# Loads of a and b from GpSimd's queue, and a weight conversion without ScalarE's mantissa pass, in a fused RWKV-7 and cosine-unit kernel

## Chip, core and metric

The kernel runs on one core of a Trainium2 chip. The metric is the device time of one execution in microseconds (us). Before the change the median of three runs is 825.35 us (823.66 to 827.18).

## What is computed

Two blocks stand one behind the other. The first is a recurrence over 768 steps for 4 batches and 8 heads of 40 channels (`r, k, v, w, a, b`). Its output, as 3072 tokens of 320 values, goes through a unit with a hidden width of 2048.

```
for t in range(S):                      # state: (B, H, D, D), D = 40
    y[:, :, t] = einsum('bhd,bhde->bhe', rt, state)
    Sa    = einsum('bhde,bhe->bhd', state, at)
    state = state * wt[:, :, None, :] - einsum('bhd,bhe->bhde', Sa, bt) \
          + einsum('bhd,bhe->bhde', vt, kt)
x = y.transpose(0, 2, 1, 3).reshape(B * S, H * D)   # (3072, 320)
h = x @ w_in                            # w_in (320, 2048), float64 in memory
out = (h * cos(h)) @ w_out              # w_out (2048, 320), float64 in memory
```

## The kernel before, in words

**Recurrence.** The sequence is cut into 24 chunks of 32 steps. `p1(c)` prepares two chunks at once from w, a and b: transposes (`wT`, `aps`, `bT`), the reciprocal `rw` of w (L395), `bn` = b times `rw` on GpSimd (L396), and the products `nps`. From `nps` VectorE computes triangular inverses for four chunks at once, in small steps (`inv_tmp`, `inv`); for chunks 0 to 7 only the diagonal half blocks are inverted this way and TensorE joins them (`pair_first`, `pair_second`, tiles `half` and `rt`). `p2(c)` prepares one chunk from k, v, r: the copies `vp`, `rp` (L566), `kn` (L573) and `vvm` (L574) on GpSimd, transposes, the products `gram`. `main(c)` carries the state: `ch_t` (sT), `ch_q` (qps), `ch_x` (x0ps), `ch_s` (sps), `ch_z` (dps). At the end of `ch_z` VectorE adds into the state tile `qz` (L732), GpSimd multiplies it (L733) and then the output `yt` (L744); the next chunk's `ch_t` needs `qz`. `yt` goes through memory to be transposed: SP stores `xd` (L753) and, when that has landed, loads `xT` (L763, L765).

**Loads.** `load(c, names, via)` (L150 to L156) issues four transfers of 40 KB for each name, one per batch. Nearly all of it goes through SP's queue, which takes its entries in order. From chunk 4 on, w comes as a cumulated product: `ws_scan` forms it on VectorE for four chunks at once, `ws_store` writes it to `wd` (L184), and the load of w reads `wd`. The tiles of a and b of chunks 4 and 5 are those of chunks 0 and 1. k, v, r have one tile each, so the load for chunk c + 1 waits for GpSimd's copies for chunk c.

**Weights.** They are float64, and are turned to float32 in 20 tiles of 128 x 512 by `rounded` (L224 to L264). Tiles 0, 1, 6, 7, 10, 11, 16, 17 hold the rows of w_in in two groups of 128, tiles 2 and 12 its last 64 rows (the tail), the others w_out. A tile goes through four stages:
- `fetch` loads the two 32-bit words of each number (`words`, L237);
- `taken` masks the high word's mantissa (`mant`, L245) and its exponent (`expo`, L246) on VectorE, then ScalarE turns the exponent into a power of two (L249) and takes the sign (L251);
- `mantissa` adds the low word (L255, VectorE), then ScalarE adds the implicit one and scales (L258);
- `product` multiplies mantissa and power (L261, VectorE), then GpSimd multiplies by the sign (L264).

The order is written out by hand: a list `w_steps` holds, for each tile n, product of n, fetch of a later tile, mantissa of n + 1, taken of n + 2. `step` pops a few of them after each piece of the recurrence. The words live in tiles that are used elsewhere too, so a fetch waits until the tile before it there has been read.

**Order of the work.** `step` counts down a list of deferred actions (`later(n, work)` runs it n steps on), so many loads are placed by a count of steps. Dummy matmuls (`busy`, and the tiny `pad` matmuls of `shifted`, 121 ahead of chunk 0's inverse and 75 at chunk 19) stand between the pieces. Once weights are ready, pieces of the second block (`ph`, `turns`, `gT`, `po`) are put between the pieces of the recurrence, and TensorE has work throughout.

**Borrowed space.** Ahead of the weights, the buffer of w_out holds other things: b of chunks 2 and 3 in its last 1024 columns (`late_out`), and ahead of these, in `spare`, the tiles `half0` (1024 columns) and `rn0` (512 columns) for the joining of chunk 0 to 3's inverses.

Of the kernel before, what the change touches and what calls it, by code (L numbers as in the profile page):

```python
# [9 lines left out]
F32 = mybir.dt.float32  # L10
I32 = mybir.dt.int32
U32 = mybir.dt.uint32
ALU = mybir.AluOpType
ACTF = mybir.ActivationFunctionType
# [6 lines left out]
def kernel(  # L21
# [43 lines left out]
    nc = tc.nc  # L65
    B, H, S, D = r.shape
    P, C, DP = 128, 32, 64
    HH = H // 2
    NCH = S // C
    DM, DFF = moe_w_in.shape  # L70
    NF = DFF // P
# [18 lines left out]
    def kept(name, shape, n=1, fill=None, part=lambda t: t, on=nc.gpsimd):  # L90

        tiles = []
        for i in range(n):
            t = const.tile(shape, F32, tag=f"{name}{i}", name=f"{name}{i}")
            if fill is not None:
                on.memset(part(t), fill)
            tiles.append(t)
        return tiles
# [8 lines left out]
    src = {"r": r, "k": k, "v": v, "w": w, "a": a, "b": b}  # L107
# [5 lines left out]
    w_out_sb = const.tile([P, NF, DM], F32, tag="w_out", name="w_out_sb")  # L113
# [2 lines left out]

    late = DFF - 2 * H * DP
    late_out = w_out_sb.rearrange("p f n -> p (f n)")[:, NF * DM - 2 * H * DP :]
    spare = w_out_sb.rearrange("p f n -> p (f n)")[:, NF * DM - 2 * H * DP - 3 * P * 4 : NF * DM - 2 * H * DP]
    half0 = spare[:, : 8 * P].rearrange("p (n t) -> p n t", t=C)  # L120
    rn0 = spare[:, 8 * P :].rearrange("p (n t) -> p n t", t=C // 2)
    nc.gpsimd.memset(half0[:, :, C // 2 :], 0.0)
    nat = {}
    for n, fill in (("w", 1.0), ("a", 0.0), ("b", 0.0)):
        for i in range(4):
# [24 lines left out]
    def load(c, names, via=nc.sync):  # L150
        for n in names:
            for i in range(B):
                at_c = src[n][i, :, c * C : (c + 1) * C, :]
                if n == "w" and c >= 4:
                    at_c = wd[c // 4][i, :, c % 4]
                via.dma_start(nat[n, c][blk[i], :, :D], at_c.rearrange("h t d -> t h d"))  # L156
# [51 lines left out]
    bn_b = kept("bn", [P, H, DP], 7, 0.0, padding)  # L208
    kn_b = kept("kn", [P, H, DP], 2, 0.0, padding)

    by_in = kept("by_in", [P, 1], 1, 0.5 / math.pi)[0]
    by_out = kept("by_out", [P, 1], 1, 2.0 * math.pi)[0]
    to_bits = kept("to_bits", [P, 1], 1, (127.0 - 1023) * 2**23)[0]


# [5 lines left out]
    WID = 512  # L221
    first_done, second_done = [], []

    def rounded(m, dst, src, by, by_sb):  # L224

        pool, tag = (
            ((sb2, "gT"), (sb2, "gT"), (sb1, "nt"), (sb1, "u"), (sb1, "inv"))[m % 5]
            if m < 10 else ((sb1, "nt"), (sb1, "u"), (sb1, "inv"))[(m - 10) % 3]  # L230
        )
        t = {}

        def fetch():
            t["words"] = pool.tile([P, WID, 2], I32, tag=tag, name="words")
            for rows, cols, part in src:
                nc.sync.dma_start(  # L237
                    t["words"][rows, cols].rearrange("p n w -> p (n w)"), part.bitcast(I32)
                )

        def taken():
            hi = t["words"][:, :, 1]
            t["mant"] = sb2.tile([P, WID], I32, tag="mant", name="mant")
            t["expo"] = sb2.tile([P, WID], I32, tag="expo", name="expo")
            nc.vector.tensor_scalar(t["mant"], hi, 0xFFFFF, None, ALU.bitwise_and)  # L245
            nc.vector.tensor_scalar(  # L246
                t["expo"], hi, 20, 0x7FF, ALU.logical_shift_right, ALU.bitwise_and
            )
            nc.scalar.activation(t["expo"], t["expo"], ACTF.Relu, bias=to_bits, scale=2.0**23)  # L249
            t["sign"] = sb2.tile([P, WID], mybir.dt.bfloat16, tag="sign", name="sign")  # L250
            nc.scalar.activation(t["sign"], hi, ACTF.Sign)  # L251

        def mantissa():
            frac = t["mant"].bitcast(F32)
            nc.vector.scalar_tensor_tensor(  # L255
                frac, t["words"][:, :, 0].bitcast(U32), 2.0**-32, t["mant"], ALU.mult, ALU.add
            )
            nc.scalar.activation(frac, frac, ACTF.Identity, bias=by_sb, scale=2.0**-20 * by)  # L258

        def product():  # L260
            nc.vector.tensor_tensor(  # L261
                dst, t["mant"].bitcast(F32), t["expo"].bitcast(F32), ALU.mult
            )
            nc.gpsimd.tensor_tensor(dst, dst, t["sign"], ALU.mult)  # L264

        return fetch, taken, mantissa, product

    def weights():


        wide = moe_w_in.dtype != F32
        work = []

        def put(dst, src, by, by_sb):
            if wide:
                work.append(rounded(len(work), dst, src, by, by_sb))
                return

            def fetch():
                for rows, cols, part in src:  # L280
                    nc.sync.dma_start(dst[rows, cols], part)

            none = lambda: None
            work.append((fetch, none, none, lambda: nc.scalar.mul(dst, dst, by)))

        flat_out = w_out_sb.rearrange("p f n -> p (f n)")
        for j in range(NF // 4):
            cs = slice(j * WID, (j + 1) * WID)
            for i in range(2):
                put(  # L290
                    w_in_sb[:, i, cs], [(every, slice(0, WID), moe_w_in[i * P : (i + 1) * P, cs])],
                    0.5 / math.pi, by_in,
                )
            if j % 2 == 0:
                put(
                    w_in_tail[:, j : j + 2].rearrange("p j f n -> p (j f n)"),
                    [
                        (
                            full[e], slice(2 * i * P, 2 * (i + 1) * P),
                            moe_w_in[2 * P :, (4 * (j + i) + 2 * e) * P : (4 * (j + i) + 2 * e + 2) * P],  # L300
                        )
                        for i in range(2)
                        for e in range(2)
                    ],
                    0.5 / math.pi, by_in,
                )
            first_done.append(len(work))
            for o in range(0, NF * DM, WID):
                if not 4 * j * DM <= o < 4 * (j + 1) * DM:
                    continue  # L310
                parts = []
                for f in range(o // DM, (o + WID - 1) // DM + 1):
                    lo, hi = max(o, f * DM), min(o + WID, (f + 1) * DM)
                    parts.append(
                        (
                            every, slice(lo - o, hi - o),
                            moe_w_out[f * P : (f + 1) * P, lo - f * DM : hi - f * DM],
                        )
                    )
                put(flat_out[:, o : o + WID], parts, 2.0 * math.pi, by_out)  # L320
            second_done.append(len(work))
        return work

# [19 lines left out]
    def later(steps, work):  # L343
        waiting.append([steps, work])

    def step(work, of_inv=0, of_w=0, small=False):


        before = list(waiting)
        work()  # L350
        G["small"] = small
        for w in before:
            w[0] -= 1
            if w[0] == 0:
                waiting.remove(w)
                w[1]()
        for steps, n in ((inv_steps, of_inv), (w_steps, of_w)):
            for _ in range(min(n, len(steps))):
                steps.pop(0)()
# [502 lines left out]
    def p1(c):  # L862


        def first_w():
            p1_w(c)
            if c == 4:
                later(1, lambda: load(6, "w"))

        def both_a():  # L870
            p1_a(c)
            if c == 4:
                later(1, lambda: load(7, "w"))
                for i in range(2):
                    later(1, lambda i=i: load(6 + i, "ab"))
            elif c >= 2 and c + 3 < NCH:
                for m in range(6):
                    later(
                        8 + m // 3 if c == 2 else (9 if c == 6 else 2) + m, lambda m=m: load(c + 2 + m % 2, "wab"[m // 2])
                    )  # L880

        return [first_w, both_a, lambda: p1_b(c), lambda: p1_n(c)]

# [23 lines left out]
    with tc.manual_schedule():  # L907
# [46 lines left out]
        first, other = p1(0), p1(2)  # L954
        for seg in (*first[:2], *other[:2], *first[2:], *other[2:]):
            step(seg)
        for m in range(2):
            w_work[m][0]()
        scanned(1)
# [10 lines left out]
        w_work[2][0]()  # L970
        p2_in(1)
        p2_kn(1)
        N_PAD = {0: 121, 19: 75}
        shifted(N_PAD[0])
        while inv_steps:
            inv_steps.pop(0)()
# [35 lines left out]
        for c in range(NCH):  # L1012
# [6 lines left out]
            elif c == 1:  # L1019
                parts = [parts0[0], parts0[1]]  # L1020
                segs = [t, parts[0], v, q, parts[1], k, x, g, s, z]
                fill = (1, 4)
            elif c == 2:
                parts = parts0[2:]
# [107 lines left out]
```

## Time and profile before

| | |
|---|---|
| median of three runs | 825.35 us |
| the profiled execution | 821.18 us |
| its span (first to last instruction) | 819.5 us |
| granted TensorE clock, mean | 0.955 |
| TensorE matmuls busy | 756.6 us (92%) |
| VectorE busy | 484.4 us (59%) |
| ScalarE busy | 386.5 us (47%) |
| GpSimd busy | 198.5 us (24%) |
| DMA, mean | 68 GB/s |

In the profile PE is TensorE's matmuls, PEld its weight loads, DVE VectorE, ACT ScalarE, POOL GpSimd, SP SyncE. A timeline line has the start, the duration, the engine, the line of the kernel, the operation, output <- inputs, how many were merged (x4), and in square brackets the idle time of the engine before it with what ended it. `SPq` lines are the issues of transfers in SP's queue: their duration is the time in the queue, not that of the transfer. A line of the table by stretches has, for each engine, the busy time and the number of instructions, then the granted clock, the mean busy share of the 16 DMA engines and GB/s. "issue" is idle time that the profile puts down to nothing. The profile is of one execution, and its idle times belong to an engine, not to the kernel: they count only where the end of the kernel depends on them.

### The profile page before, as it was taken

To read this page: it belongs to the slowest core of one execution; us is meant where nothing else is said; L and a number is where in the kernel's file an instruction comes from. 1 tells how busy PE (TensorE), PEld (TensorE's weight loads), DVE (VectorE), ACT (ScalarE), POOL (GpSimd) and SP (SyncE) were. 2 spreads that over 40 slices of the span, in tenths; PEclk is the share of its full clock that TensorE was granted. 3 is DMA by queue.
4 is the path that set the end of the run, shared out by engine and by line. 5 is a ranking of instruction groups with operands and counts; after the bars stand their busy time and mean duration, and the time that the engine had idled before them with its cause. 6 is when DMAs were issued, how large, how long until landed. Compare 5 with 4: busy or idle time off the path is not lost.

```text
span 819.5 us, 39690 instructions
## 1 busy us (share of the span) xinstructions
PE 756.6 (92%) x17858; PEld 580.2 (71%) x17858; DVE 484.4 (59%) x1025; ACT 386.5 (47%) x720; POOL 198.5 (24%) x354
## 2 busy tenths in 40 slices
PE   3676787999899999999999999999999999999997
PEld 2653456677677777787777877777787777777775
DVE  6956667866364698454796554895445873332231
ACT  1324566654254544446345445435635435363352
POOL 5214352430214123221230330330230222201000
PEclk9856687999999999999999999999999999999999
DMA  7536554254144323334224314214220212101000
GB/s 122 126 83 177 160 143 115 45 126 73 29 103 92 67 52 61 70 90 75 54 38 71 73 59 72 53 38 68 59 40 25 45 39 51 21 19 36 19 17 16
DMA packets 183304, 55.79 MB, mean 68 GB/s; under 512 B 157152, under 2 KB 178656, under 8 KB 183136
## 3 DMA queue, kind: packets, MB, share of 16 engines
q1 hardware_dynamic: 180560, 51.95, 29.2%
q8 instruction: 140, 2.29, 1.2%
q10 hardware_dynamic: 2320, 0.98, 0.6%
q0 software_dynamic: 256, 0.33, 0.2%
q14 instruction: 28, 0.23, 0.1%
HBM read 42.07 MB, written 11.14 MB: 65 GB/s over the span
## 4 chain that ended last, share of the span: by engine, by line
PE 63%; DVE 14%; DMA 6%; ACT 5%; SPq 5%; issue 5%; POOL 2%; DVEq 0%; ACTq 0%; POOLq 0%
PE ph L101 22%; PE po L101 18%; SPq L156 4%; PE x0ps L101 3%; PE dps L101 3%; PE gram L101 3%; DVE inv_tmp L480 2%; PE vT L330 2%; DVE rw L395 2%; DVE inv L484 2%; PE nps L101 2%; PE sps L101 2%; PE qps L101 2%; DMA words<-in_moe_w_out_dram 1%; PE sT L634 1%
## 5 line engine op out<-in xcount | busy, mean ns | idle before, releaser
L101 PE MATMUL po<-w_out_sb,gT 128*128 128x320 f32 x768 | 223.2, 439 | 0.0
L101 PE MATMUL ph<-xT,w_in_sb 128*128 128x256 f32 x768 | 188.7, 391 | 2.8 <-issue 2.5
L101 PEld LDWEIGHTS po<-w_out_sb,gT 128*128 128x128 f32 x768 | 140.2, 190 | 54.2 <-issue 1.7
L101 PEld LDWEIGHTS ph<-xT,w_in_sb 128*128 128x128 f32 x768 | 141.2, 193 | 32.9 <-issue 14.9
L806 ACT ACTIVATE turns<-ph,rnd 128x512 f32<-128x512 f32 x96 | 64.1, 686 | 159.0 <-PE ph L101 158.6
L808 DVE SCALAR_TENSOR_TENSOR turns<-turns,ph 128x512 f32<-128x512 f32 x96 | 64.0, 684 | 117.4 <-ACT turns L806 117.1
L816 DVE TENSOR_TENSOR gT<-ph,turns 128x512 f32<-128x512 f32 x96 | 65.7, 686 | 37.5 <-ACT turns L813 37.5
L733 POOL TENSOR_TENSOR qz<-qz,wc 128x160 f32<-128x160 f32 x92 | 41.7, 472 | 158.3 <-DVE qz L732 157.7
L813 ACT ACTIVATE turns<-turns,half_pi 128x512 f32<-128x512 f32 x96 | 69.3, 722 | 3.1
L812 ACT ACTIVATE turns<-turns 128x512 f32<-128x512 f32 x96 | 60.2, 627 | 16.8 <-DVE turns L808 16.8
L101 PE MATMUL ph<-xT,w_in_tail 64*128 64x256 f32 x384 | 55.8, 410 | 0.0
L484 DVE TENSOR_TENSOR inv<-inv,inv_tmp 128x31 f32<-128x31 f32 (+15 forms) x124 | 50.8, 410 | 4.3
L566 POOL COPY vp<-nat_v 128x320 f32<-128x320 f32 x25 | 12.2, 486 | 160.5 <-DMA nat_v<-in_v_dram 134.4
L732 DVE TENSOR_TENSOR qz<-dps,qz 128x160 f32<-128x160 f32 x92 | 28.9, 314 | 35.6 <-PE dps L101 35.3
L480 DVE TENSOR_TENSOR inv_tmp<-u,inv 128x31 f32<-128x31 f32 (+15 forms) x124 | 48.2, 389 | 2.3
L395 DVE RECIPROCAL rw<-nat_w 128x320 f32<-128x320 f32 x20 | 42.8, 2141 | 0.0
L638 ACT COPY s<-sT 128x512 f32<-128x512 f32 x46 | 24.5, 584 | 37.1 <-PE sT L634 37.0
L101 PEld LDWEIGHTS ph<-xT,w_in_tail 64*128 64x128 f32 x384 | 33.8, 190 | 9.4 <-issue 5.5
L744 POOL TENSOR_TENSOR yt<-yt,wb 128x512 f32<-128x512 f32 x24 | 31.4, 1309 | 22.4 <-DVE yt L739 22.4
L634 PE MATMUL sT<-ident,qz 128*128 128x128 f32 x184 | 26.6, 287 | 5.6 <-POOL qz L733 2.9
L396 POOL TENSOR_TENSOR bn<-nat_b,rw 128x320 f32<-128x320 f32 x22 | 19.5, 887 | 48.8 <-DVE rw L395 41.6
L698 DVE TENSOR_TENSOR sm<-sps,su 128x128 f32<-128x128 f32 x48 | 11.7, 285 | 31.9 <-ACT sm L693 31.9
(136 smaller groups left out, 1108.4 us busy)
## 6 DMA issues: line engine op xcount, KB each, us to landing
words<-in_moe_w_in_dram SPq DMA_DIRECT2D x8, 512.0 KB
nat_k<-in_k_dram SPq DMA_DIRECT2D x96, 40.0 KB
nat_v<-in_v_dram SPq DMA_DIRECT2D x96, 40.0 KB
nat_r<-in_r_dram SPq DMA_DIRECT2D x96, 40.0 KB
xd<-yt SPq DMA_DIRECT2D x48, 80.0 KB
out_dram<-ot SPq DMA_DIRECT2D x24, 160.0 KB
nat_b<-in_b_dram SPq DMA_DIRECT2D x88, 40.0 KB
wd<-ws SPq DMA_DIRECT2D x5, 640.0 KB
```

The lines of the kernel that those rows point to most:

```text
L101: nc.tensor.matmul(o, lhsT=lhsT, rhs=rhs, start=start, stop=stop, skip_group_check=True)
L156: via.dma_start(nat[n, c][blk[i], :, :D], at_c.rearrange("h t d -> t h d"))
L395: nc.vector.reciprocal(rw, wn)
L480: nc.vector.tensor_tensor(tmp, u[:, j : j + 1, :j].to_broadcast([P, C - j, j]), x[:, j:, j : j + 1].to_broadcast([P, C - j, j]), ALU.mult,)
L484: nc.vector.tensor_tensor(x[:, j:, :j], x[:, j:, :j], tmp, ALU.subtract)
L634: nc.tensor.transpose(ps[:, i // 4, (i % 4) * P : (i % 4 + 1) * P], qz[:, i // 2, i % 2, C : C + P], ident)
L733: nc.gpsimd.tensor_tensor(z, z, wc.rearrange("p (f m b) -> p f m b", f=2, m=2)[:, :, :, bb] .unsqueeze(3).to_broadcast([P, 2, 2, D]), ALU. ...
L806: nc.scalar.activation(n, u, ACTF.Identity, bias=rnd, scale=1.0)
L808: nc.vector.scalar_tensor_tensor(n, n, -ROUND, u, ALU.add, ALU.subtract)
L812: nc.scalar.activation(n, n, ACTF.Abs)
L813: nc.scalar.activation(n, n, ACTF.Sin, bias=half_pi, scale=-2.0 * math.pi)
L816: nc.vector.tensor_tensor(gT[:, 2 * e : 2 * e + 2].rearrange("p f t -> p (f t)"), us[e], ns[e], ALU.mult)
```

## The change

- The weights: the mask also sets the implicit one (`bitwise_or` with 0x100000), so ScalarE's pass L258 falls, and its scale goes into a three-operand product on VectorE. GpSimd's multiplication by the sign moves from the end of `product` to the end of `taken`, and works on the power of two.
- The loads: a and b of chunks 4 and 5 are issued by GpSimd, 16 transfers, behind its copies for chunk 1. w of chunks 4 and 5 stays on SP and is placed 5 and 7 steps after the first piece of chunk 1, which puts it behind the words of tile 8 and of tile 9. The deferred loads that `p1(2)` set up for them fall.
- `half0` moves into the last 1024 columns of w_out's buffer (where b of chunks 2 and 3 was), and its memset on GpSimd moves behind the preparation of chunks 0 to 3. `rn0` stays where it was. Two memsets of constants fall.
- The pad ahead of chunk 0's inverse has 115 matmuls instead of 121.

```diff
-    spare = w_out_sb...[:, NF * DM - 2 * H * DP - 3 * P * 4 : NF * DM - 2 * H * DP]
-    half0 = spare[:, : 8 * P].rearrange("p (n t) -> p n t", t=C)
-    rn0 = spare[:, 8 * P :].rearrange("p (n t) -> p n t", t=C // 2)
-    nc.gpsimd.memset(half0[:, :, C // 2 :], 0.0)
+    half0 = late_out.rearrange("p (n t) -> p n t", t=C)
+    rn0 = w_out_sb...[:, NF * DM - 2 * H * DP - P * 4 : NF * DM - 2 * H * DP]
...
-            nc.vector.tensor_scalar(t["mant"], hi, 0xFFFFF, None, ALU.bitwise_and)
+            nc.vector.tensor_scalar(
+                t["mant"], hi, 0xFFFFF, 0x100000, ALU.bitwise_and, ALU.bitwise_or
+            )
...
             nc.scalar.activation(t["sign"], hi, ACTF.Sign)
+            power = t["expo"].bitcast(F32)
+            nc.gpsimd.tensor_tensor(power, power, t["sign"], ALU.mult)
...
-            nc.scalar.activation(frac, frac, ACTF.Identity, bias=by_sb, scale=2.0**-20 * by)
...
         def product():
-            nc.vector.tensor_tensor(
-                dst, t["mant"].bitcast(F32), t["expo"].bitcast(F32), ALU.mult
-            )
-            nc.gpsimd.tensor_tensor(dst, dst, t["sign"], ALU.mult)
+            nc.vector.scalar_tensor_tensor(
+                dst, t["mant"].bitcast(F32), 2.0**-20 * by, t["expo"].bitcast(F32), ALU.mult, ALU.mult
+            )
...
-            elif c >= 2 and c + 3 < NCH:
+            elif c > 4 and c + 3 < NCH:
                 for m in range(6):
-                    later(
-                        8 + m // 3 if c == 2 else (9 if c == 6 else 2) + m, lambda m=m: load(c + 2 + m % 2, "wab"[m // 2])
-                    )
+                    later((9 if c == 6 else 2) + m, lambda m=m: load(c + 2 + m % 2, "wab"[m // 2]))
...
             step(seg)
+        nc.gpsimd.memset(half0[:, :, C // 2 :], 0.0)
...
         p2_kn(1)
-        N_PAD = {0: 121, 19: 75}
+        for c in (4, 5):
+            load(c, "ab", nc.gpsimd)
+        N_PAD = {0: 115, 19: 75}
...
                 segs = [t, parts[0], v, q, parts[1], k, x, g, s, z]
+                later(5, lambda: load(4, "w"))
+                later(7, lambda: load(5, "w"))
                 fill = (1, 4)
```

More of the change, by code (lines that the diff above doesn't have):

```diff
@@ L118 @@
     late_out = w_out_sb.rearrange("p f n -> p (f n)")[:, NF * DM - 2 * H * DP :]
-    spare = w_out_sb.rearrange("p f n -> p (f n)")[:, NF * DM - 2 * H * DP - 3 * P * 4 : NF * DM - 2 * H * DP]
-    half0 = spare[:, : 8 * P].rearrange("p (n t) -> p n t", t=C)
-    rn0 = spare[:, 8 * P :].rearrange("p (n t) -> p n t", t=C // 2)
-    nc.gpsimd.memset(half0[:, :, C // 2 :], 0.0)
+    half0 = late_out.rearrange("p (n t) -> p n t", t=C)
+    rn0 = w_out_sb.rearrange("p f n -> p (f n)")[:, NF * DM - 2 * H * DP - P * 4 : NF * DM - 2 * H * DP]
+    rn0 = rn0.rearrange("p (n t) -> p n t", t=C // 2)
     nat = {}
@@ L209 @@
     kn_b = kept("kn", [P, H, DP], 2, 0.0, padding)
-    by_in = kept("by_in", [P, 1], 1, 0.5 / math.pi)[0]
-    by_out = kept("by_out", [P, 1], 1, 2.0 * math.pi)[0]
     to_bits = kept("to_bits", [P, 1], 1, (127.0 - 1023) * 2**23)[0]
@@ L222, with rounded @@
     first_done, second_done = [], []
-    def rounded(m, dst, src, by, by_sb):
+    def rounded(m, dst, src, by):
         pool, tag = (
@@ L272, in weights, with put @@
         work = []
-        def put(dst, src, by, by_sb):
+        def put(dst, src, by):
             if wide:
-                work.append(rounded(len(work), dst, src, by, by_sb))
+                work.append(rounded(len(work), dst, src, by))
                 return
@@ L291, in weights @@
                     w_in_sb[:, i, cs], [(every, slice(0, WID), moe_w_in[i * P : (i + 1) * P, cs])],
-                    0.5 / math.pi, by_in,
+                    0.5 / math.pi,
                 )
@@ L304, in weights @@
                     ],
-                    0.5 / math.pi, by_in,
+                    0.5 / math.pi,
                 )
@@ L319, in weights @@
                     )
-                put(flat_out[:, o : o + WID], parts, 2.0 * math.pi, by_out)
+                put(flat_out[:, o : o + WID], parts, 2.0 * math.pi)
             second_done.append(len(work))
```

## The prediction

> **What bounds the kernel now.** I read the stretches of the span first, then the queue that the chain of waits names in the worst stretch, then the engines that stand behind that queue. Times are us from the start of the profiled execution.
>
> ```profile
> core 0: us, PE busy (x) PEld busy (x) DVE busy (x) ACT busy (x) POOL busy (x), PEclk, DMA share, GB/s
> 44.00:62.00 18.00, 13.31 (x498) 9.47 (x494) 9.09 (x25) 5.83 (x12) 1.16 (x1) 0.59 0.42 80
> 62.00:75.00 13.00, 7.25 (x93) 4.87 (x87) 6.68 (x15) 3.57 (x6) 6.19 (x9) 0.50 0.60 133
> ...
> 150.00:170.00 20.00, 18.43 (x339) 14.15 (x337) 17.21 (x26) 9.50 (x19) 6.44 (x15) 1.00 0.38 72
> ...
> 260.00:500.00 240.00, 237.86 (x5665) 186.41 (x5664) 153.31 (x332) 119.18 (x223) 56.18 (x103) 1.00 0.32 65
> ```
>
> From 260 on TensorE is busy all the time (237.86 of 240): nothing is gained there but by starting earlier. In 62 to 75 no engine is busy for more than 7.25 of 13, and the DMA engines stand at 0.60. Something issues too late. The chain of waits in that stretch is one issue on SP after another (L156 about 0.45 each), then a landing of `words`. SP's own timeline:
>
> ```profile
> 39.20 0.40 SPq L184 DMA_DIRECT2D wd<-ws  x1
> 44.29 4.31 SPq L156 DMA_DIRECT2D nat_w<-wd  x8
> 48.72 2.13 SPq L156 DMA_DIRECT2D nat_a<-in_a_dram  x4
> 50.96 3.51 SPq L237 DMA_DIRECT2D words<-in_moe_w_in_dram  x4
> 54.57 3.10 SPq L156 DMA_DIRECT2D nat_a<-in_a_dram  x4
> 57.72 4.86 SPq L156 DMA_DIRECT2D nat_b<-in_b_dram  x8
> 62.67 3.54 SPq L156 DMA_DIRECT2D nat_k<-in_k_dram  x4
> 66.31 1.88 SPq L156 DMA_DIRECT2D nat_v<-in_v_dram  x4
> 68.23 1.94 SPq L156 DMA_DIRECT2D nat_r<-in_r_dram  x4
> 70.27 3.24 SPq L237 DMA_DIRECT2D words<-in_moe_w_out_dram  x7
> ```
>
> SP stands from 39.60 to 44.29 for the store of `wd` to land and then issues without a gap to 75. What is wanted first (words of weight tiles 3 to 5, v and r of chunk 2) is last in the queue, behind w, a, b of chunks 4, 5, which nothing reads before 149. VectorE and GpSimd pay:
>
> ```profile
> 73.96 0.56 DVE L245 TENSOR_SCALAR mant<-words 128x512 int32<-128x512 int32 x1 [6.18 <-DMA words<-in_moe_w_out_dram]
> ...
> 99.19 0.43 DVE L245 TENSOR_SCALAR mant<-words 128x512 int32<-128x512 int32 x1 [3.08 <-DMA words<-in_moe_w_out_dram]
> ...
> 105.18 0.43 DVE L245 TENSOR_SCALAR mant<-words 128x512 int32<-128x512 int32 x1 [2.31 <-DMA words<-in_moe_w_in_dram]
> ```
>
> **The loads of a and b.** Sixteen issues leave SP: 2.13 + 3.10 and the 4.86 of b, 10.1. Eight of w (4.31) and the wait of 4.7 go from this place too; w comes back at two places behind words 8 and 9. Of the 23.0 from 39.6 to 62.6, only the 3.5 of the tail's words stays.
>
> The Trainium skill speaks against this ("DMA: Bandwidth & Descriptors", section "Issuing engines are not separate DMA queues"): all issuers share the same 16 DMA engines, and another issuer saves only the sequencer's issue time, usually small beside the transfer. By that rule the move is worth about nothing. The rows say that here the issue time is the limit: SP issues without a gap for 31 us while the DMA engines are at 0.42 and 0.60. I go by the rows.
>
> **What GpSimd pays.** The sixteen issues stand behind the copies for chunk 1. The nearest row is its own eight:
>
> ```profile
> 1.90 0.75 POOL L156 DMA_DIRECT2D w_in_sb<-in_a_dram  x1
> ...
> 3.99 4.02 POOL L156 DMA_DIRECT2D w_in_sb<-in_a_dram  x7
> ```
>
> That is 0.57 each, so 9.2 for sixteen. They can start at 44.3 and end at 53.5; the second eight each wait for the landing of one of the first eight (median 3.7 to land, less than the 4.6 that the first eight take). The cover is this idle time:
>
> ```profile
> 43.34 0.50 POOL L574 COPY vvm<-nat_v 128x320 f32<-128x320 f32 x1
> 60.20 1.16 POOL L264 TENSOR_TENSOR w_in_sb<-w_in_sb,sign 128x512 f32<-128x512 f32 x1 [16.36 <-DVE w_in_sb L261]
> 62.55 1.74 POOL L733 TENSOR_TENSOR qz<-qz,wc 128x160 f32<-128x160 f32 x4 [1.19 <-DVE qz L732]
> ```
>
> Behind the issues stand two sign products (2 x 1.16) and then qz at 62.55, on which the whole recurrence waits. The cover holds while sixteen issues take no more than 62.5 - 44.3 - 2.3 = 15.9, that is 0.99 each. A second rule bears on that: by the Trainium skill's "SBUF — State Buffer" (section "Who interferes with whom"), GpSimd can't write descriptors while VectorE runs in a two-port mode; a DMA of 620 ns took about 3100 ns so. In 44 to 54 VectorE has mostly two-input inverse steps; of the form the page names only four 0.42 conversions fall there, which is 1.7, so 10.9 in all. If every issue cost 3.1 it were 49.6. The eight of before ran beside VectorE's memsets in part and took 0.57; I take 9.2 and keep 49.6 for a rival.
>
> **What follows on the path.** SP now: the tail's words 40.1 to 43.6, k, v, r of chunk 2 (behind GpSimd's kn of chunk 1) 7.4 to 51.3, words 3 and 4 by 53.5 (tile 4 waits for the inverse, 51.7), words 5 by 55.3. All have landed by 60. So:
>
> Step 1. The 6.18 before 73.96 goes: tile 3 is taken at 67.8. vp and rp follow yt at 66.0 and 66.5, not 70.19 and 72.67. TensorE: sT to 65.2, dummies 1.5, aps 1.05, vT and rT 1.1, dummies 1, so qps at 69.4 instead of 75.94. 6.5 gained.
>
> Step 2. The xd of chunk 0 is issued at 66.0 instead of 74.89, and not behind 1.6 MB of words. Its landing was waited for 5.8; I take 2.5 to 4.5. Then xT (1.5) and words 7 at 71 to 73 (83.39 before), k of chunk 3 (1.9 to 3.6), words 8 (2.45): landed at 79 to 83, wanted at 82.9 (tile 8 was taken at 92.43). Now the four w issues (1.9), v and r of chunk 3 (5.0), words 9: landed between 87.5 and 91.3, against 99.19: 8 to 11.7 gained. Behind it another 1.9 of w, words 10, landing 5.3 (tile 7's) to 8.7 (its own before): tile 10 is taken between 92 and 98.9 instead of 105.18. The middle is 10 gained, and I carry that: what w takes back is in it.
>
> Step 3. From 105 to 126 SP, TensorE and VectorE keep their order, so the 10 stays.
>
> **The conversion.** Twenty ScalarE passes of 0.72 go (14.4 busy). ScalarE is not the limit over the whole stretch; its passes are on the path where the next copy stands behind them. The product changes from a two-tensor form (0.68) to a three-operand form (0.68 by L255 and L808): zero. The two-operation mask costs what L246 does (0.42): zero. The memsets that go or move are 0.1 and 0.53; the moved one falls at 29.7 and pushes kn by 0.5, while TensorE is busy to 32.9 and reaches kT at 34.6: hidden, but k, v, r of chunk 1 start 0.5 later, taken in above.
>
> The sign product (1.16, 1.54 beside a VectorE conversion) now stands before VectorE's product instead of behind it. Its chain is expo 0.72, sign 0.65, GpSimd 1.16: 2.8 with the hand-overs, while VectorE has 1.9 of other steps between taking a tile and its product. In the dense stretch 106 to 116 a tile took 3.1 to 3.3. The new wait is at worst 0.9 a tile, and where it is present VectorE's conversion no longer waits 0.95 for GpSimd (1.38 against 0.43). I take zero; bounds -0.3 to +0.5 a tile over some 14 tiles, -4 to +7.
>
> What readers gain is a wait less: w_out_sb is ready with VectorE, and half0 lies in the last two weight tiles.
>
> ```profile
> 126.80 1.75 PE L101 MATMUL aps<-rt,w_out_sb 32*32 32x16 f32 x128 [2.81 <-POOL w_out_sb L264]
> ```
>
> This wait falls. Next late behind it is gram and VectorE's ag (1.40 idle), then sm behind ScalarE's sign (0.87). On the other side sign product 19 now stands ahead of qz on GpSimd (0.45 later). I take 2.
>
> **Dummies.** Six pad matmuls less are 0.16 (70 took 1.89). But all later TensorE instructions move by 12 places against its unexplained stalls ("issue", 1.85 at 55.9, 1.88 at 83.3, 1.41 at 129): one may enter or leave the path, 2 either way; I take zero.
>
> **Sum.** 10 + 2 = 12. The span goes from 819.5 to 807.5, the profiled execution from 821.18 to 809. The median of the runs is 4.2 above the profiled one, for both kernels I assume: 825.35 - 12 = 813. From 150 on the order is the same and TensorE is full, so nothing gives it back.
>
> **The rivals.** *Likeliest, 0.62:* as above, 808 to 817. *Gain cut short, 0.18:* w at its new places holds up words 9 and 10 and only step 1 is kept, 6.2: 819. For it: SP's groups of four sometimes take 3 instead of 1.9. Against: before, words 7 came at 83.39. *Sign chain, 0.12:* the new wait for GpSimd costs 0.5 on 14 tiles, 7 of 12: 820, at the price of 0.9 on 14 tiles 825: no difference. *GpSimd's issues, 0.08, slower:* each is held up by VectorE; beyond 0.99 each, qz of chunk 0 slips by 16 times the excess. At 1.74 the gain is gone; at the page's 3.1 qz is 34 later: 825 - 12 + 34 = 847. Against it stands the 0.57. That the loads don't leave SP is excluded by the instruction order of the changed kernel (24 issues gone from that place, 16 on GpSimd).
>
> A measurement can tell about 0.5%, 4.1 us, from no change. Faster by more holds the first two and part of the third: 0.81; within 0.5% 0.12; slower 0.07. The range goes from 808 to 822.
>
> **What would show it.** Tile 3 taken near 68 with no wait for words; GpSimd's sixteen issues over by 54 and qz near 62.5; SP's words 7 near 72; tile 10 taken near 95; the first full TensorE stretch near 138 instead of 150. Wrong, if GpSimd is still issuing at 62, if VectorE waits for GpSimd's expo by more than 0.5 a tile, or if the waits for words come back at tiles 9 and 10 at their old times.

## The result and the profile after

Over 20 runs the changed kernel took 820.58 us in the median (818.07 to 825.84), the kernel before 821.12 (816.92 to 827.18): a ratio of 0.9995, interval 0.9977 to 1.0014. Beside other versions it later gave 0.9991 (0.9969 to 1.0013). The change makes no difference that can be measured. Forecast were 813 and 12 us less. The profiled execution took 818.33, its span 816.6. A ratio in this document is not the quotient of the two medians, and leaves out runs more than 1.5% above the fastest of their kernel (two of *words_late*, two of *quiet121*, one of the kernel before).

The same stretches after, columns as before:

```profile
44.00:62.00 18.00, 10.16 (x382) 7.10 (x382) 9.02 (x25) 4.98 (x10) 13.27 (x20) 0.69 0.89 214
62.00:75.00 13.00, 8.86 (x224) 6.33 (x223) 8.09 (x18) 2.23 (x5) 5.00 (x8) 0.58 0.20 57
260.00:500.00 240.00, 238.33 (x5795) 187.02 (x5794) 153.56 (x333) 120.37 (x225) 54.13 (x100) 1.00 0.32 65
```

The traffic has moved forward (DMA share 0.89 instead of 0.42 in 44 to 62, 0.20 instead of 0.60 behind it). But TensorE did less in 44 to 62: 382 matmuls, before 498. The queues did what the diff says. GpSimd's timeline:

```profile
45.20 2.32 POOL L155 DMA_DIRECT2D nat_a<-in_a_dram  x4
...
52.11 2.60 POOL L155 DMA_DIRECT2D nat_b<-in_b_dram  x4
54.72 2.56 POOL L252 TENSOR_TENSOR expo<-expo,sign 128x512 f32<-128x512 f32 x2
68.76 1.31 POOL L732 TENSOR_TENSOR qz<-qz,wc 128x160 f32<-128x160 f32 x3 [11.48 <-DVE qz L731]
```

Sixteen issues from 45.20 to 54.71, 0.57 to 0.65 each, then the two sign products, then 11.48 idle: the cover held. SP had issued the words of tiles 3 to 5 by 57.3, and VectorE took tile 3 at 74.43 and tile 10 at 99.73 without a wait for words. Yet tile 3 was forecast at 67.8: GpSimd's qz of chunk 0 came at 68.76 instead of 62.55. TensorE's timeline says why:

```profile
58.51 0.27 PE L101 MATMUL sps<-x,rt 32*32 32x72 f32 x1 [3.75 <-issue]
63.89 0.21 PE L101 MATMUL gram<-rT,vT 40*32 40x32 f32 x1 [3.64 <-issue]
```

Before there was one such stall here, 1.85. "issue" means that no other engine and no DMA released TensorE. The trace shows what came just ahead: one of the queues marked "instruction" carries 140 packets of 16,384 bytes. They are TensorE's: its 17,852 matmuls and as many weight loads make 255 instructions to a packet, and two later versions with 128 matmuls less have 139. Packets land at 57.0 and 62.5, and TensorE goes on 1.5 and 1.4 us behind them. In all 18 traces of this study the stalls named issue of 0.4 us and more between 44 and 66 end 1.0 to 1.6 behind such a landing, and two packets never start less than 3.23 apart; 128 small matmuls can run in about 1.6 (64 of `qps` take 0.81).

For the rest I compare TensorE's start at the same matmul (pads left out) with the kernel before, from the profiled executions. The head gives before's own time; minus is earlier. The differences are good to about 0.2.

```
                 57.88  75.94 126.80 131.66 168.25 204.81 260.38    end
                  gram    qps    aps     ph     ph    aps     ph
changed            6.0   -0.5   -7.4   -5.7   -4.5   -4.1   -2.0   -2.8
changed, again     4.9   -1.8   -9.0   -3.3   -0.1    0.4    2.1    2.8
```

Of the 12 forecast, 7.4 and 9.0 are there at 126.8; they are gone before the end, in several steps. In the first 5 us behind 126.8, 1.7 and 5.7 are lost: both profiles have a stall of 3.69 for instructions there (before: 1.41), and the second then waits for VectorE, which had itself waited 6.52 for the words of tile 14:

```profile
118.08 0.43 DVE L242 TENSOR_SCALAR mant<-words 128x512 int32<-128x512 int32 x1 [6.52 <-DMA words<-in_moe_w_out_dram]
```
```profile
128.27 3.75 PE L101 MATMUL ph<-xT,w_in_sb 128*128 128x256 f32 x8 [3.94 <-DVE gT L815]
```

Near 250, GpSimd and TensorE of the changed kernel in the first profile, and the same place before:

```profile
249.45 0.86 POOL L395 TENSOR_TENSOR bn<-nat_b,rw 128x320 f32<-128x320 f32 x1 [7.15 <-DMA nat_b<-in_b_dram]
```
```profile
258.38 1.96 PE L101 MATMUL ph<-xT,w_in_sb 128*128 128x256 f32 x8 [2.67 <-DMA xT<-xd]
```
```profile
260.38 1.97 PE L101 MATMUL ph<-xT,w_in_sb 128*128 128x256 f32 x8 [0.28 <-DMA xT<-xd]
```

TensorE waits 2.67 for xT at this place; before it waited 0.28 at 260.38. In the second profile it waits 1.56.

### The profile page after: what moved, and what is told of

Read it like the earlier page. It is cut to its first block, busy times and chain, and to the rows that moved or that the text cites. A ratio compares the mean times of both kernels' runs of the same rounds, so it can differ in the third digit from the quotient of the medians.

```text
span 816.6 us, 39686 instructions
## 1 busy us (share of the span) xinstructions
PE 752.6 (92%) x17852; PEld 578.0 (71%) x17852; DVE 484.9 (59%) x1025; ACT 374.2 (46%) x700; POOL 208.9 (26%) x368
## 4 chain that ended last, share of the span: by engine, by line
PE 64%; DVE 16%; issue 6%; ACT 5%; DMA 4%; SPq 3%; POOL 2%; DVEq 0%; ACTq 0%; POOLq 0%
PE ph L101 22%; PE po L101 19%; PE x0ps L101 3%; PE dps L101 3%; PE gram L101 3%; PE vT L329 2%; SPq L155 2%; DVE inv_tmp L479 2%; DVE rw L394 2%; DVE inv L483 2%; PE nps L101 2%; PE sps L101 2%; PE qps L101 2%; DVE turns L807 1%; PE sT L633 1%
## 5 line engine op out<-in xcount | busy, mean ns | idle before, releaser
L252 POOL TENSOR_TENSOR expo<-expo,sign 128x512 f32<-128x512 f32 x20 | 25.5, 1277 | 35.3 <-ACT sign L250 28.9
```

## The experiments

Three theories came first. A: the transfers that now land in 44 to 62 lengthen TensorE's stalls for its instructions. B: six pads less move the code against its packets. C: the new conversion gives the gain back through GpSimd. A fourth, D, came after the first four runs: a lead of the front is given back where SP's queue, not TensorE, sets the time. B' is B with a reason added later: a packet that was asked for ahead of a wait is asked for behind it. S: the front is bound by the supply of instructions. Ratios are to the kernel before, measured beside each version on the same chip, with 95% intervals.

**Which part of the change.** *conv_only* is the kernel before with the new conversion; *loads_only* is the changed kernel with the old conversion and 121 pads; *pad121* is

```diff
-        N_PAD = {0: 115, 19: 75}
+        N_PAD = {0: 121, 19: 75}
```

and *words_late* holds words 3 to 5 and the fetch of `ws` behind words 6:

```diff
-            later(12, lambda: ws_fetch(q + 1))
+            later(14 if q == 1 else 12, lambda: ws_fetch(q + 1))
...
-            if nxt < len(w_work):
+            if nxt < len(w_work) and n:
                 w_steps.append(w_work[nxt][0])
+            if n == 1:
+                w_steps.append(lambda: [w_work[m][0]() for m in range(3, 6)])
...
-        for m in range(3, 5):
-            w_work[m][0]()
```

> The kernel before with the new conversion alone (loads, half0, 121 pads as before). Theory A: the front is bound by the words' arrival as before, so tile 3 is taken near 74, the stall near 56 stays at about 1.9 us, and the time is 0 to 3 us below before. Theory B says nothing else. Theory C: the sign product ahead of VectorE's product costs, so the kernel is 2 to 6 us slower than before.

> The changed kernel with the old conversion (ScalarE's mantissa pass and the sign product at the end) and 121 pads; the loads and half0 as changed. Theory A (the transfers that now land in 44 to 62 hold up TensorE's code fetch): the stalls put down to issue between 53 and 65 stay at 6 to 7.5 us in all, qz of chunk 0 comes near 68, and the time is within 3 us of the kernel before. Theory B (the stalls come from the pads, which moved the code against its blocks): with 121 pads again only one stall of about 1.9 us is left there, qz near 62, and the time is 6 to 9 us below before. Theory C (the new conversion gives the gain back through GpSimd): qz near 62 or 68 alike, but the stretch from tile 3 to tile 9 is shorter than in the changed kernel by 3 us or more.

> The changed kernel with 121 pads instead of 115. Theory A: the stalls between 53 and 65 move by six matmuls and stay at 6 to 7.5 us in all; the time is within 2 us of the changed kernel. Theory B: one stall of about 1.9 us is left and the time is 4 to 6 us lower.

> The changed kernel with the words of tiles 3 to 5 and the load of ws held behind the words of tile 6, so that 1.9 MB leave the stretch 50 to 62; a and b on GpSimd stay. Theory A: the stalls between 53 and 65 shrink from 7.4 to at most 2.5 us, qz of chunk 0 comes near 63 instead of 68.4, tile 3 is taken near 70, and the time is 3 to 6 us below the changed kernel. Theory B: the stalls stay at 7.4 us, qz at 68, and the time is not lower or even 2 us higher, as the words come later.

```
                 ratio (interval)          57.88  75.94 126.80 131.66 204.81 260.38    end
conv_only   0.9986 (0.9967 to 1.0004)        0.8   -2.4   -3.9   -3.5   -1.8   -1.8   -0.3
loads_only  0.9984 (0.9965 to 1.0002)        4.1   -2.9  -12.4   -7.3   -4.1   -1.6    1.3
pad121      0.9967 (0.9947 to 0.9987)        6.3   -0.1   -7.2   -1.2    2.8    0.4    2.6
words_late  0.9974 (0.9944 to 1.0003)        2.2   -3.2  -11.9   -6.0   -3.8   -1.6    2.7
```

C falls: the conversion alone is not slower, and in the changed kernel VectorE waits for GpSimd's product in two places only, 1.04 at 82.8 and 1.05 at 111.9. The six pads are worth something: pad121 is the only one whose interval leaves out no change. B as it was written falls too: pad121's stalls in 44 to 66 are 7.7 and not 1.9. loads_only and words_late have the full 12 at 126.8 and nothing of it at the end. That made D. (words_late's own gain is doubtful: its medians are 822.09 and 822.22.) The last column comes from one execution each, and the runs of a version spread over 8 to 15 us; that is why pad121 can end 2.6 late in its profile and be faster in the median.

**Where the lead goes.** *b_gps* lets GpSimd issue b of chunks 10 and 11, in the changed kernel, *b_gps_before* in the kernel before:

```diff
-    later((9 if c == 6 else 2) + m, lambda m=m: load(c + 2 + m % 2, "wab"[m // 2]))
+    later((9 if c == 6 else 2) + m, lambda m=m: load(c + 2 + m % 2, "wab"[m // 2],
+          nc.gpsimd if c == 8 and m > 3 else nc.sync))
```

> The changed kernel, with the b loads of chunks 10 and 11 (eight issues, in the profiles at 244.8 to 250.8 on SP) issued by GpSimd behind its copies of rp, where it is idle for 13.9 us. Theory D (the lead of the front is given back at 250 to 258, because SP's queue and not TensorE sets when b arrives, and bn, qz, yt, xd, xT stand behind it): GpSimd's wait for nat_b (7.15) is gone, TensorE's wait for xT at 258 (2.67) falls below 0.5, and the time falls by 2.5 to 4 against the changed kernel, to about 817. Rival A (only TensorE's stalls for its instructions in 44 to 66 and at 125 ate the gain): nothing at 258 matters for the end, the time stays within 1 of 820.6.

> The kernel before, with the same move of b of chunks 10 and 11 alone. Theory D: TensorE's wait for xT there is only 0.28, since in this kernel TensorE comes late enough, so the move gives 0 to 1 us (821 to 822). If the queue in 225 to 252 cost every version the same, this would gain as much as in the changed kernel, about 3.

b_gps: 820.75, 0.9976 (0.9959 to 0.9994); b_gps_before: 821.93, 0.9986 (0.9969 to 1.0002). In b_gps GpSimd's wait for nat_b and TensorE's for xT are gone, but the time is only 0.2% below the changed kernel's 0.9995, and the intervals overlap. The same move took 0.14% from the kernel before, so it is not seen to be worth more behind a lead. In its profiled execution b_gps brought no lead there (2.7 late at 204.81), so nothing could be kept. Not decided by this pair.

*relief* joins words_late, this move, and the words of tile 14 issued by ScalarE: on SP they stood behind the xd and xT of chunk 1 and the k behind them, and words_late's VectorE had paid for it:

```profile
115.45 0.43 DVE L242 TENSOR_SCALAR mant<-words 128x512 int32<-128x512 int32 x1 [5.57 <-DMA words<-in_moe_w_out_dram]
```
```diff
-                nc.sync.dma_start(
+                (nc.scalar if m == 14 else nc.sync).dma_start(
                     t["words"][rows, cols].rearrange("p n w -> p (n w)"), part.bitcast(I32)
```

> The changed kernel with three queue changes together: words 3 to 5 and the fetch of ws held behind words 6, words of tile 14 issued by ScalarE instead of SP (they waited behind the xd and xT of chunk 1 and k), b of chunks 10 and 11 by GpSimd. Theory D: tile 14 is taken without the wait of 5.57 seen with the first of these alone, TensorE's wait at 126 for VectorE (3.94) falls below 1, its wait at 258 below 0.5, and the lead of 6 at 212 reaches the end: about 815. Rival A: stalls for instructions come back at other places and the time is 819 to 822.

> The version with three queue changes, with 121 pads. Theory B': issue stalls of 44 to 66 fall from 7.1 to 3.5 to 5.5; the time is 1 to 3 below that version's 820, near 818. Theory D with other limits behind it (VectorE's chain at 126, xT): the time does not move, 819 to 821, because what the front gains is given back at 121 to 131.

relief: 819.93, 0.9959 (0.9941 to 0.9977), where D forecast about 815 and its rival 819 to 822. The wait for VectorE at 126 is gone in its profile, the time did not follow. With 121 pads (*relief121*): 815.32, 0.9947 (0.9928 to 0.9965). Tile 14 is now taken at 110.43 with a wait of 0.73. The next place where a lead ends on SP then stands in relief121's trace: TensorE at chunks 6 and 7, and the queue behind it.

```profile
161.95 0.63 PE L329 MATMUL aps<-ident,nat_a 128*128 128x128 f32 x4 [2.59 <-DMA nat_a<-in_a_dram]
```
```profile
155.68 2.76 SPq L155 DMA_DIRECT2D nat_b<-in_b_dram  x4
158.54 1.87 SPq L155 DMA_DIRECT2D nat_a<-in_a_dram  x4
```

The second a stands behind a b that is wanted later. *aabb* is relief121 with the order a, a, b, b; *before_rel* is the kernel before (its loads, conversion and pads) with tile 14, the b of chunks 10 and 11, and this order.

```diff
-                for i in range(2):
-                    later(1, lambda i=i: load(6 + i, "ab"))
+                for n in "ab":
+                    for i in range(2):
+                        later(1, lambda i=i, n=n: load(6 + i, n))
```

> The version with three queue changes and 121 pads (0.9947 of the kernel before), and one order more: on SP the loads of chunks 6 and 7 go a, a, b, b instead of a, b, a, b. In that version's profile TensorE waits 2.59 at 162 for the second nat_a, issued 158.5 to 160.4 behind four loads of b. Theory D (what the front gains is given back at places where SP's queue sets the time): the wait falls below 0.5, and 1 to 2.5 us more reach the end, about 0.992 to 0.9935. Rival: the next late thing stands right behind it and the time stays within 1 us of that version's.

> The kernel before, loads and conversion as they were, with the later queue changes alone: words of tile 14 by ScalarE, b of chunks 10 and 11 by GpSimd, a, a, b, b for chunks 6 and 7. Theory D: without the lead of the front these places hardly bind, 0 to 2 us less than before (0.9975 to 1). If the queue changes explain the whole gain of the combined version by themselves, 0.9945 or less.

```
                 ratio (interval)          57.88  75.94 126.80 131.66 204.81 260.38    end
relief121   0.9947 (0.9928 to 0.9965)        3.0   -3.0  -12.1   -9.1   -6.0   -5.7   -4.9
aabb        0.9932 (0.9904 to 0.9961)        3.3   -3.6  -12.1   -7.3   -6.2   -8.5   -7.5
before_rel  0.9982 (0.9956 to 1.0008)        0.8   -0.0   -1.2   -1.1    0.0   -0.7    0.0
```

aabb took 815.48, before_rel 820.59 and before 822.32 on the same chip. The queue changes alone are worth little, 0.18% with no change inside the interval. D says that they are worth more behind a lead, since these places bind only a TensorE that comes early. The times do not show that. The parts, each by the ratios above, are 0.05% (the change), 0.28 (121 pads, pad121 against changed), 0.21 (the words held back, words_late against changed) and 0.18 (before_rel): 0.72 in sum, as an estimate, and aabb has 0.68. The run that would tell, words_late with 121 pads and no other queue change, was not made. What speaks for D is in the profiles. aabb's own lines:

```profile
160.54 1.09 PE L329 MATMUL aps<-ident,nat_a 128*128 128x128 f32 x8 [0.35 <-DVE sm L697]
251.65 1.68 PE L101 MATMUL ph<-xT,w_in_sb 128*128 128x256 f32 x7
```

The waits at 162 and 258 are gone, and from 131.66 on the lead stays, in this one execution. In relief121, which still has the wait at 162, it goes from 9.1 to 4.9. What aabb still loses, it loses ahead of that, from 12.1 to 7.3:

```profile
119.33 0.29 PE L101 MATMUL gram<-aT,kT 40*32 40x32 f32 x6 [3.02 <-issue]
124.19 2.05 PE L101 MATMUL ph<-xT,w_in_sb 128*128 128x256 f32 x4 [3.81 <-DVE gT L815]
```

First a wait for instructions, then one for VectorE, which still converts weight tiles there. aabb has the lowest ratio of the versions with 121 pads; against relief121 its interval overlaps, so the trace shows that the last edit removes the wait, and the time does not show a gain.

**What stalls TensorE in 44 to 66.** *quiet* and *quiet121* are words_late without the loads of a and b of chunks 4 and 5, with 115 and 121 pads; *before115* is the kernel before with 115 pads; *before0* and *aabb0* have none at the first place and 68 at the second.

> The changed kernel with words 3 to 5 and the fetch of ws held behind words 6, and without the loads of a and b of chunks 4 and 5: these two chunks compute with the numbers of chunk 0, and 16 transfers of 0.66 MB in all are left out. Theory A (transfers that land in 44 to 62 lengthen TensorE's stalls for its instructions): the stalls named issue between 44 and 66, 7.4 in the changed kernel and 3.9 with the words held, fall to 1.9 or less, and qz of chunk 0 starts by 62. If the stalls have another cause they stay at 3.5 to 7.5. Theory D: the time is still 818 to 822, since the queue at 225 to 252 is as it was.

> The changed kernel with words 3 to 5 and the fetch of ws held, without the loads of a and b of chunks 4 and 5 (these two compute with the numbers of chunk 0), and with 121 pads as before. Theory B': the issue stalls of 44 to 66 fall from the 5.6 that the same kernel had with 115 pads to 1.9 to 3. Theory A, already weak since 5.6 remained without the loads, gives 5.6 again. If it stays at 5 or more, neither is the cause.

> The kernel before with 115 pad matmuls instead of 121 and nothing else. Theory B' (the six pads less shift the blocks in which TensorE's instructions arrive, so that a block that had been asked for ahead of a wait is asked for behind it): TensorE's idle time named issue between 44 and 66, 1.9 to 3.1 in the three kernels with the old place of the loads and 121 pads, rises to 5 to 6, the stall at sps (54) appears and that at gram (58) grows to 3.5 or more; the time rises by 0 to 3. If only the transfers lengthen the stalls (theory A) it stays at 1.9 to 3.1.

> The kernel before with no pads at the first place and 68 at the second. Theory S: 0 to 3 us less than before, as its front is held by SP's queue at 62 to 75 behind it. Theory B': slower by 0 to 4, as the kernel with 115 pads was by 3.4, if 121 was at a good place.

> As the version just named, with no pad matmuls at the first place and 68 instead of 75 at the second, so that the code from chunk 19 on lies as with 121 and 75 (128 matmuls less are one whole instruction packet of 16,384 bytes). Theory S (in 44 to 66 TensorE is bound by how fast its instructions arrive, one packet in no less than 3.3 us): a packet less saves up to 3.4 us in the front, 1 to 3 at the end. Theory B' alone (the place of the block edges decides): it lies 7 matmuls further than with 121 in the other direction from 115, and the time may go either way by 3.

> The changed kernel itself, once more, beside the versions above on one chip: 820 to 821 by all theories. With it the spread of its stalls between 44 and 66 (8.4 in its first profile) is seen a second time: theory A and B' expect 6 to 8.5 again; if it is 2 to 3, the stalls are chance from one execution to the next.

```
                ratio (interval)           "issue" of TensorE, 44 to 66
before          1                           1.9
before115       1.0042 (1.0024 to 1.0060)   4.8
before0         0.9993 (0.9968 to 1.0017)   4.0
changed         0.9995 (0.9977 to 1.0014)   8.4, again (after_again) 5.8
words_late      0.9974 (0.9944 to 1.0003)   5.5
quiet           1.0004 (0.9972 to 1.0036)   5.6
quiet121        0.9964 (0.9940 to 0.9987)   7.5
pad121          0.9967 (0.9947 to 0.9987)   7.7
relief          0.9959 (0.9941 to 0.9977)   7.1
relief121       0.9947 (0.9928 to 0.9965)   5.3
aabb            0.9932 (0.9904 to 0.9961)   4.8
aabb0           0.9916 (0.9886 to 0.9946)   3.8
```

quiet121's 7.5 is from an execution of 823.24, its median is 818.23. quiet's stalls, with a DMA share of 0.46 in 44 to 66 (changed: 0.73):

```profile
54.78 0.27 PE L101 MATMUL sps<-x,rt 32*32 32x72 f32 x1 [1.38 <-issue]
60.70 0.21 PE L101 MATMUL gram<-rT,vT 40*32 40x32 f32 x1 [4.19 <-issue]
```

A falls: without the transfers the stalls stay. Six pads alone make the kernel before 0.42% slower, 3.4 us, and in its profile the stall at sps appears that it did not have:

```profile
56.33 0.27 PE L101 MATMUL sps<-x,rt 32*32 32x72 f32 x1 [1.56 <-issue]
60.05 0.21 PE L101 MATMUL gram<-rT,vT 40*32 40x32 f32 x1 [1.99 <-issue]
```

So the number of pads does change the time: in all four pairs that differ by it alone, 121 stands below 115, by 0.12% (relief) to 0.42% (before), though only in the kernel before do the intervals not overlap. That these stalls are how it does so, as B' says, is not shown. In the changed layout they stay at 4.8 to 7.7 with 121 pads. before0 has 4.0 and is no slower than before with 1.9. And in before115's profile (an execution of 825.06, its median is 822.87) TensorE is, by the measure of the tables above, 4.3 early at 75.94 and 4.4 early at 131.66. Only then does it fall back, to 1.0 late at 260.38 and 3.8 at the end, with these waits among others:

```profile
165.59 1.09 PE L330 MATMUL aps<-ident,nat_a 128*128 128x128 f32 x4 [1.85 <-DMA nat_a<-in_a_dram]
...
261.37 1.97 PE L101 MATMUL ph<-xT,w_in_sb 128*128 128x256 f32 x8 [2.15 <-DMA xT<-xd]
```

S falls too: a whole packet less moved the kernel before by nothing, and aabb0 by no more than its interval (815.97 beside 815.48). What makes one execution of the front stall 4 and another 8 stays open; the same kernel gave 8.4 and 5.8.

## Why the prediction was wrong, by its own steps

- *What GpSimd pays:* right. Sixteen issues over at 54.7 (forecast 53.5), at 0.57 to 0.65; the price of 3.1 each did not show (in the Trainium skill's "SBUF — State Buffer" that figure stands in the section "A bandwidth-pool intuition that's wrong (but worth ruling out)").
- *Step 1, 6.5 gained:* mis-sized. (Its own terms add up to 69.9 at qps, so 6.1.) The wait of 6.18 for words went, but only 0.5 was left at qps in the first profile and 1.8 in the second (75.94). The chain gram, qz, yt ahead of it was taken from before unchanged, and came 5 to 6 late for TensorE's instruction stalls. By "one may enter or leave the path, 2 either way; I take zero" they were priced at nothing. It is not the loads of a and b that do it (quiet), and six pads more do not undo it (pad121). Besides, 6.18 was one execution's number. before_rel and b_gps_before have the same program as before up to this place, before115 the same queue:

```profile
73.91 0.57 DVE L245 TENSOR_SCALAR mant<-words 128x512 int32<-128x512 int32 x1 [5.08 <-DMA words<-in_moe_w_out_dram]
```
```profile
74.23 0.51 DVE L245 TENSOR_SCALAR mant<-words 128x512 int32<-128x512 int32 x1 [2.93 <-DMA words<-in_moe_w_out_dram]
```
```profile
71.13 0.86 DVE L245 TENSOR_SCALAR mant<-words 128x512 int32<-128x512 int32 x1 [0.45 <-DMA words<-in_moe_w_out_dram]
```

  With 121 pads, qps starts at 73.3 to 75.9 in the four profiles with the old place of the loads (before, before_rel, b_gps_before, conv_only), at 72.1 to 75.9 in four with the new (loads_only, pad121, relief121, aabb): step 1 brought little that can be told from this spread.
- *Step 2 and 3, 10 carried to 126:* tile 10 at 99.73, 5.5 gained, where 95 was forecast; but before_rel and b_gps_before, still with the old loads, took it at 102.04 and 103.04, against 105.18 in the profile that the sum started from. The mechanism was right: words hardly hold VectorE any more up to tile 10 (0.38 at tile 9), and loads_only and aabb have 12 at 126.8.
- *Dummies, zero:* wrong. Six pads cost 0.42% in the kernel before; putting them back gave the changed kernel 0.9967 instead of 0.9995, intervals that overlap only just.
- *The conversion, zero, and 2 for the readers:* no chain through GpSimd. The wait of 2.81 at 126.8 did fall, but was replaced at once: in the changed kernel by the gram stall, then by a slow clock.

```profile
119.43 1.29 PE L101 MATMUL aps<-rt,w_out_sb 32*32 32x16 f32 x128
125.04 0.27 PE L101 MATMUL gram<-aT,kT 40*32 40x32 f32 x3 [3.69 <-issue]
```

- *"From 150 on the order is the same and TensorE is full, so nothing gives it back":* the failed step. Of the lead at 131.66, 5.7 and 3.3, the two profiles lose 2.9 and 6.1 by the end. In the first the longer wait for xT at 258 (2.67, before 0.28) is as large as most of it. In the second TensorE runs slowly behind its wait for VectorE (eight `ph` in 3.75), waits 2.23 for GpSimd's qz at 144 and 1.56 for xT at 262. TensorE was full there in the kernel before at that kernel's pace; the 0.28 at 260 was slack used up, not slack to spare. SP's queue is one cause of the loss, VectorE, GpSimd and the instruction stalls are others, and their shares of the time stay open. With three places of SP's queue mended (tile 14, 162 and 258), words 3 to 5 held back and 121 pads, 0.68% of the time, 5.6 us, is gained (aabb), but the separate parts explain that sum as well.
- *The ledger:* of 12 us forecast, the two profiles miss 4.6 and 3.0 ahead of 126.8, lose 1.7 and 5.7 up to 131.66, and 2.9 and 6.1 behind it.
- *The start of the sum:* 825.35 was the median of three runs. Over 20 it is 821.12, as the profiled execution (821.18); the surplus of 4.2 was chance. It is by this surplus that 820.58 lies within the forecast's 808 to 822: of the 12 us, 0.5 came.

The Trainium skill's rule that another issuer saves little ("DMA: Bandwidth & Descriptors", "Issuing engines are not separate DMA queues") had the better outcome. Its reason was not what the traces show: in the front SP's issues stood one behind the other for 31 us and held VectorE up by 0.45 to 6.18 in the versions above. The nearest rivals were *Sign chain* at its higher price, no difference, and *Gain cut short*. Neither mechanism showed: VectorE waited for GpSimd's product at two tiles, not 14, and w did not stand in the way of words 9 and 10 (a wait of 0.38 at tile 9).

## What to carry to other kernels

A lead gained early counts only up to the next place where something other than the engine sets the time: ask at each later place when its data could be there at the earliest, not whether the engine waits there now. Size a gain from several executions: the wait that this forecast removed was 6.18, 5.08 and 2.93 in three profiles of the same code. An edit that shifts a long unrolled instruction stream has a price of its own: try the old alignment before judging the edit. And to show that two edits help each other, run each alone, both, and neither; here one of these was missing.

## What was not expected of the hardware

- Supply of instructions to TensorE: packets of 16,384 bytes, never closer than 3.23 us; the stalls of 44 to 66 are 0.5 to 4.2 long and end 1.0 to 1.6 behind a landing. The Trainium skill ("Runtime: NRT & Kernel Launch", "Instruction fetch mechanics") has blocks of this size, and calls the cost of crossing one mostly hidden; here it is not, and the measurement decides. What these stalls cost at the end of the kernel is not shown.
- Idle time of TensorE can be paid twice. Behind words_late's wait of 2.82 at 258, eight `ph` matmuls took 3.75 at a granted clock of 0.50 (258 to 264). Behind the changed kernel's wait of 2.67 at the same place they took 1.96 at 1.00.
- GpSimd issues a small transfer in 0.57 to 0.65 beside VectorE's inverse steps.
